# Splitting the first expert layer of a fused attention and mixture kernel into three single TensorE passes

## The chip, the cores and the metric

The kernel runs on one core of one Trainium2 chip. The metric is the device time of one execution in microseconds (us). A single execution carries 1 or 2 us more than the profiled span, which runs from the first to the last instruction. In the lines of the profile PE is TensorE, PEld its weight loads, DVE VectorE, ACT ScalarE, POOL GpSimd, and L12 is line 12 of the kernel.

## The reference, cut to what matters

A gated linear attention over 768 steps (4 batches, 8 heads of 48) gives `x` with 3072 rows of 384. Four experts then work on every row:

```python
p = domain_probs / (domain_probs.sum(-1, keepdims=True) + 1e-09)
for e in range(E):                              # E = 4
    h = np.maximum(x @ w1[e], 0.0)              # 384 -> 1024, the layer that the change rewrites
    out += p[:, e:e + 1] * (h @ w2[e])          # 1024 -> 384
```

All inputs are float32.

## The kernel before

The rows are handled in seven token groups: two of 256 rows (groups 0 and 1) and five of 512. While the experts of one group run, the attention of the next group is interleaved with them, a piece at a time. An "up" is one 128-row block of the first layer, a "down" is one 128-row block of the second. All weights are loaded once and stay in SBUF.

```python
w1_sb = const.tile([P, E, KC, F], F32, name="w1_sb")
w2_sb = const.tile([P, E, FCH, DM], F32, name="w2_sb")
...
def up(gi, e, fc):
    n = len(groups[gi]) * P                      # 256 or 512
    ...
    hps = ps.tile([P, NT], F32, name="hps", tag="g")
    for kc in range(KC):                         # KC = 3
        nc.tensor.matmul(hps[:, :n], lhsT=w1_sb[:, e, kc, fc * P:(fc + 1) * P],
                         rhs=xTs[gi][:, kc, :n], start=(kc == 0), stop=(kc == KC - 1))
    nc.scalar.activation(out=hidden[gi, e][:, fc, :n], in_=hps[:, :n], func=ACT.Relu)

def down(gi, e, slot):
    ...
    ops = ps.tile([P, DM], F32, name="ops", tag="o")          # two buffers
    for fc in range(FCH):                        # FCH = 8
        nc.tensor.matmul(ops, lhsT=hT[:, fc, slot * P:(slot + 1) * P], rhs=w2_sb[:, e, fc, :], ...)
    # VectorE: acc = ops * prob + acc; after the last expert, DMA to out
```

One of seven levels of an attention unit looks as follows. TensorE computes the scores, then VectorE updates `QT`, `KT` and the decays. The next level's scores need those three, so a level is a chain TensorE, VectorE, TensorE.

```python
for li, m in enumerate(LEVELS):
    # 8 small matmuls sc <- KT, QT (16 instructions in the profile)
    nc.vector.tensor_mul(qv[:, :, :, 1, :], qv[:, :, :, 1, :], spread(left))    # QT
    nc.vector.tensor_mul(kv[:, :, :, 0, :], kv[:, :, :, 0, :], spread(right))   # KT
    nc.vector.tensor_mul(dec, left, right)
    # two copy_predicated lat <- sc
    yield                                        # here other work is placed between
```

## Time and profile before

The median of three runs was 1429.11 us (1428.98 to 1430.6); the profiled execution spans 1426.1 us.

| stage | length, us | TensorE busy, us | granted clock |
|---|---|---|---|
| prologue (attention of the first two units, loads) | 77.6 | 50.0 | 0.63 |
| group 0 (256 rows) | 103.4 | 101.3 | 1.00 |
| group 1 (256 rows) | 173.8 | 158.1 | 0.92 |
| groups 2 to 5 together (512 rows each) | 882.0 | 876.2 | 1.00 |
| group 6 (512 rows, no attention beside it) | 189.3 | 185.7 | 1.00 |

How to read it: length less busy time is TensorE's idle time. The clock is the mean that the throttle granted, 1.00 being full speed; where a trace has no record of it, the views show 1.00. Busy time is not a fixed quantity, because the same instructions are busy longer at half clock.

### The profile page before, as it was taken

Reading aid. Unit: us, or ns where it says so; the run is one execution under the profiler, and the core shown is the slowest. Engines: PE = TensorE matmul, PEld = TensorE weight load, DVE = VectorE, ACT = ScalarE, POOL = GpSimd, SP = SyncE. Lnnn points to the kernel's source line nnn. Section 1 sums busy time; section 2 is a strip of 40 time slices with the busy share of each in tenths; the row PEclk is TensorE's granted clock in tenths of the full one; section 3 lists DMA queues with packets and bytes.
Section 4 is the critical chain, followed back from the end, with each engine's and each line's share of the span. In section 5 each row is a group of like instructions: output and inputs, shape, how many; then the busy total and the mean of one; then the engine's idle time right before and its main releaser. Section 6 shows DMA issues by size and latency. Waiting matters only on the chain.

```text
span 1426.1 us, 16040 instructions
## 1 busy us (share of the span) xinstructions
PE 1371.2 (96%) x6712; PEld 858.4 (60%) x6712; DVE 421.7 (30%) x1086; ACT 169.0 (12%) x317; POOL 55.8 (4%) x128
## 2 busy tenths in 40 slices
PE   5799989989999999999999999999999999999998
PEld 4677776667556556566566565565565565555555
DVE  4343244433332322333323223323233233000001
ACT  1021111110110110110101101101101011101110
POOL 2000000000000000000000000000000000000000
PEclk7599998998999999999999999999999999999999
DMA  9421002110020010020110020100001000000000
GB/s 312 130 45 23 1 7 50 23 23 6 7 45 6 18 23 5 2 62 0 23 23 1 6 50 12 23 6 18 6 18 28 1 1 1 0 23 0 0 0 23
DMA packets 112504, 37.39 MB, mean 26 GB/s; under 512 B 103600, under 2 KB 110896, under 8 KB 112432
## 3 DMA queue, kind: packets, MB, share of 16 engines
q1 hardware_dynamic: 109056, 36.18, 10.1%
q8 instruction: 54, 0.88, 0.3%
q10 hardware_dynamic: 3376, 0.17, 0.2%
q14 instruction: 18, 0.15, 0.0%
HBM read 31.63 MB, written 4.72 MB: 25 GB/s over the span
## 4 chain that ended last, share of the span: by engine, by line
PE 95%; DVE 3%; issue 1%; DMA 0%; SPq 0%; ACT 0%; ACTq 0%
PE hps L226 36%; PE ops L235 35%; PE sc L162 14%; PE tp L128 3%; PE yps L187 3%; PE yps L184 1%; PE sps L198 1%; DVE lat L174 1%; DVE KT L169 1%; PE xps L215 1%; DVE QT L168 0%; DMA ra<-in_alpha_dram 0%; DVE dec L171 0%; SPq L102 0%; ACT xT L216 0%
## 5 line engine op out<-in xcount | busy, mean ns | idle before, releaser
L226 PE MATMUL hps<-xT,w_sb 128*128 128x512 f32 (+1 forms) x1344 | 543.1, 546 | 1.7 <-ACT xT L216 1.7
L235 PE MATMUL ops<-w_sb,hT 128*128 128x384 f32 x1536 | 510.8, 488 | 0.0
L235 PEld LDWEIGHTS ops<-w_sb,hT 128*128 128x128 f32 x1536 | 286.6, 190 | 188.5 <-issue 2.4
L226 PEld LDWEIGHTS hps<-xT,w_sb 128*128 128x128 f32 x1344 | 244.9, 192 | 191.5 <-issue 169.3
L162 PEld LDWEIGHTS sc<-QT,KT 48*128 48x128 f32 x2688 | 190.5, 202 | 135.2 <-issue 132.0
L162 PE MATMUL sc<-QT,KT 48*128 48x64 f32 x2688 | 215.4, 294 | 34.4 <-DVE lat L174 34.4
L228 ACT ACTIVATE hT<-hps 128x512 f32<-128x512 f32 (+1 forms) x224 | 120.2, 536 | 782.0 <-PE hps L226 782.0
L243 DVE SCALAR_TENSOR_TENSOR acc<-ops,p_all,acc 128x384 f32<-128x384 f32 x72 | 44.5, 618 | 391.4 <-PE ops L235 391.4
L174 DVE COPY_PREDICATED lat<-masks,sc 128x256 f32<-128x256 uint8 x336 | 152.7, 519 | 0.0
L168 DVE TENSOR_TENSOR QT<-QT,dec 128x256 f32<-128x256 f32 x144 | 61.3, 426 | 263.5 <-PE sc L162 263.5
L151 POOL TENSOR_TENSOR own<-rv,dot 128x384 f32<-128x384 f32 x24 | 19.9, 830 | 1049.8 <-DVE dot L150 942.2
L169 DVE TENSOR_TENSOR KT<-KT,dec 128x256 f32<-128x256 f32 x144 | 60.3, 419 | 0.0
L187 PE MATMUL yps<-rv,lat 128*128 128x48 f32 x384 | 56.4, 278 | 0.0
L187 PEld LDWEIGHTS yps<-rv,lat 128*128 128x128 f32 x384 | 52.9, 204 | 0.2
L240 DVE TENSOR_SCALAR acc<-ops,p_all 128x384 f32<-128x384 f32 x24 | 14.8, 618 | 124.8 <-PE ops L235 124.8
L194 ACT COPY AT<-tp 128x512 f32<-128x512 f32 x20 | 11.7, 586 | 281.6 <-PE tp L128 281.4
L144 DVE TENSOR_TENSOR QT<-tp,AT 128x512 f32<-128x512 f32 x24 | 16.6, 692 | 85.8 <-PE tp L128 85.8
L184 PE MATMUL yps<-st,QT 128*128 128x96 f32 x160 | 32.8, 286 | 0.0
L189 DVE TENSOR_TENSOR own<-own,yps 128x384 f32<-128x384 f32 x24 | 13.3, 554 | 64.0 <-PE yps L187 64.0
L184 PEld LDWEIGHTS yps<-st,QT 128*128 128x128 f32 x160 | 25.8, 192 | 5.5 <-issue 2.4
L171 DVE TENSOR_TENSOR dec<-dec 128x128 f32<-128x128 f32 (+3 forms) x144 | 28.1, 195 | 0.0
L149 POOL TENSOR_TENSOR own<-rq,rk 128x384 f32<-128x384 f32 x24 | 24.6, 1024 | 64.6 <-PE xps L215 60.3
(36 smaller groups left out, 301.3 us busy)
## 6 DMA issues: line engine op xcount, KB each, us to landing
w_sb<-in_moe_w_dram SPq DMA_DIRECT2D x8, 1536.0 KB, 16.2
ra<-in_alpha_dram SPq DMA_DIRECT2D x24, 192.0 KB, 2.8
rk<-in_k_dram SPq DMA_DIRECT2D x24, 192.0 KB, 3.3
rq<-in_q_dram SPq DMA_DIRECT2D x24, 192.0 KB, 3.4
rv<-in_v_dram SPq DMA_DIRECT2D x24, 192.0 KB, 2.7
out_dram<-acc SPq DMA_DIRECT2D x24, 192.0 KB, 1.9
ident<-ident_c ACTq DMA_DIRECT2D x1, 64.0 KB, 1.8
masks<-masks_c ACTq DMA_DIRECT2D x1, 56.0 KB, 2.5
```

Source lines behind the costliest of these rows:

```text
L128: nc.tensor.transpose(tp[:, p, :], src(p), ident)
L162: nc.tensor.matmul(sc[i][:, p, :], lhsT=KT[rows, p, :], rhs=qv[rows, p, :, 1, :], start=True, stop=True)
L168: nc.vector.tensor_mul(qv[:, :, :, 1, :], qv[:, :, :, 1, :], spread(left))
L169: nc.vector.tensor_mul(kv[:, :, :, 0, :], kv[:, :, :, 0, :], spread(right))
L171: nc.vector.tensor_mul(dec, left, right)
L174: nc.vector.copy_predicated(halves(lat[:, i], m)[:, :, :, 1, :], mk.unsqueeze(1).broadcast_to([P, NP, nb, m]), sc[i].rearrange("p a (b r) ...
L184: nc.tensor.matmul(yps[:, p], lhsT=QT[:, p, :], rhs=st[:, p], start=True, stop=False)
L187: nc.tensor.matmul(yps[:, p, i, :], lhsT=lat[:, i, p, :], rhs=rv[:, 2 * p + i, :], start=(cb == 0), stop=(cb == 0 or i == 1))
L226: nc.tensor.matmul(hps[:, :n], lhsT=w1_sb[:, e, kc, fc * P:(fc + 1) * P], rhs=xTs[gi][:, kc, :n], start=(kc == 0), stop=(kc == KC - 1))
L228: nc.scalar.activation(out=hidden[gi, e][:, fc, :n], in_=hps[:, :n], func=ACT.Relu)
L235: nc.tensor.matmul(ops, lhsT=hT[:, fc, slot * P:(slot + 1) * P], rhs=w2_sb[:, e, fc, :], start=(fc == 0), stop=(fc == FCH - 1))
L243: nc.vector.scalar_tensor_tensor(out=acc, in0=ops, scalar=prob, in1=acc, op0=ALU.mult, op1=ALU.add)
```

## The change

A float32 matmul of 512 columns takes 2 x 429 ns in this kernel. The change computes the same product from three single passes whose operands fit the narrower single-pass form (float32r in the code). Write x = H + L and w = A + B, where H and A are the values with their low 12 bits cleared. The kernel keeps A, 4096·B and A - 4096·B of the weights, and H, L and H/4096 - L of x. It accumulates `one` = A·H + 4096·B·L and `two` = (A - 4096·B)·(H/4096 - L). Then `one`·(1 + 1/4096) - `two` is, apart from rounding, A·H + A·L + B·H + B·L: four products for three multiplications.

The price: w1 grows threefold and no longer fits in SBUF beside everything else. So each half expert (a "piece") is split on chip once, written to DRAM as `kept`, and read back for every later group; w2 is read from DRAM each time too. The core of the diff (cuts marked):

```diff
+    def split_weights(i):
+        w = w1t[i] = wts.tile([P, 3, KC, FH], F32R, name="w1")      # wts: two buffers
+        r = staged.pop(i)
+        top = wts.tile([P, KC, FH], F32, name="w_top", bufs=1)
+        nc.scalar.activation(out=r, in_=r, func=ACT.Copy, scale=4096.0)
+        clear_low(top, r)                                           # VectorE bit mask
+        nc.scalar.activation(out=w[:, 0], in_=top, func=ACT.Copy, scale=1 / 4096.0)
+        nc.gpsimd.tensor_sub(w[:, 1], r, top)
+        nc.gpsimd.tensor_sub(w[:, 2], w[:, 0].bitcast(F32), w[:, 1].bitcast(F32))
+        nc.sync.dma_start(out=kept[i], in_=w.bitcast(F32))
+    def load_w1(i):
+        if i < NPC:                                                 # the 8 pieces of the first group
+            split_weights(i)
+        elif i < NPC * len(groups):
+            w = w1t[i] = wts.tile([P, 3, KC, FH], F32R, name="w1")
+            nc.sync.dma_start(out=w.bitcast(F32), in_=kept[i % NPC])
...  # attention: x is split the same way, one ScalarE and three VectorE operations a unit
     def up(gi, e, fc):
...
+        if f == 0:                                                  # first of a piece's four ups
+            if i > 0:
+                stage(i + 3)
+                load_w1(i + 1)
...
-        for kc in range(KC):
-            nc.tensor.matmul(hps[:, :n], lhsT=w1_sb[:, e, kc, fc * P:(fc + 1) * P], ...
-        nc.scalar.activation(out=hidden[gi, e][:, fc, :n], in_=hps[:, :n], func=ACT.Relu)
+        for out, parts in ((one, (1, 0)), (two, (2,))):
+            for part in parts:
+                for kc in range(KC):
+                    nc.tensor.matmul(out, lhsT=w1t[i][:, part, kc, col], ...
+        nc.scalar.activation(out=t, in_=one, func=ACT.Copy, scale=1 + 1 / 4096.0)
+        nc.vector.tensor_sub(hT, t, two)
...  # relu on ScalarE, one up later
+        if f == FPH - 1:
+            del w1t[i]
     def down(gi, e, slot):
-        ops = ps.tile([P, DM], F32, name="ops", tag="o")
+        ops = ps.tile([P, DM], F32, name="ops", tag="o", bufs=1)
```

More of the change, by code (lines that the diff above doesn't have):

```diff
@@ L11 @@
 F32 = mybir.dt.float32
+F32R = mybir.dt.float32r
+U32 = mybir.dt.uint32
 U8 = mybir.dt.uint8
@@ L54 @@
     NT = B * P
+    HALVES = 2
+    FH = F // HALVES
+    FPH = FCH // HALVES
+    NPC = E * HALVES
     LEVELS = [1 << i for i in range(7)]
@@ L66 @@
     const = ctx.enter_context(tc.tile_pool(name="const", bufs=1))
-    raw = ctx.enter_context(tc.tile_pool(name="raw", bufs=3))
+    wts = ctx.enter_context(tc.tile_pool(name="wts", bufs=2))
+    dram = ctx.enter_context(tc.tile_pool(name="dram", bufs=1, space=bass.MemoryType.DRAM))
     work = ctx.enter_context(tc.tile_pool(name="work", bufs=2))
@@ L73 @@
     masks = const.tile([P, len(LEVELS), HALF], U8, name="masks")
-    w1_sb = const.tile([P, E, KC, F], F32, name="w1_sb")
-    w2_sb = const.tile([P, E, FCH, DM], F32, name="w2_sb")
     NBLK = B * NCB
@@ L87, with load @@
     place = {u: (gi, i) for gi, g in enumerate(groups) for i, u in enumerate(g)}
-    raws = {}
+    srcs = {"a": alpha, "k": k, "q": q, "v": v}
+    raws = [{nm: const.tile([P, H, D if nm == "v" else HD], F32, name=f"r{nm}{i}")
+             for nm in srcs} for i in range(2)]
     xTs = {}
     hidden = {}
+    relus = deque()
     accs = {}
-    def load(u):
+    def load(u, names):
         if u >= len(units):
@@ L97, in load @@
         cb, b = units[u]
-        for nm, src in (("a", alpha), ("k", k), ("q", q)):
-            t = raw.tile([P, NP, 2, HD], F32, name=f"r{nm}")
-            flat = t.rearrange("p a b c -> p (a b) c")
-            nc.gpsimd.memset(flat[:, :, D:], 0.0)
+        for nm in names:
             nc.sync.dma_start(
-                out=flat[:, :, :D],
-                in_=src[b, :, cb * P:(cb + 1) * P, :].rearrange("h s d -> s h d"))
-            raws[u, nm] = t
-        t = raw.tile([P, H, D], F32, name="rv")
@@ L107, in load @@
-        nc.sync.dma_start(
-            out=t, in_=v[b, :, cb * P:(cb + 1) * P, :].rearrange("h s d -> s h d"))
-        raws[u, "v"] = t
-    def load_weights(e):
-        nc.sync.dma_start(out=w1_sb[:, e], in_=moe_w1[e].rearrange("(c p) f -> p c f", p=P))
-        nc.sync.dma_start(out=w2_sb[:, e], in_=moe_w2[e].rearrange("(c p) d -> p c d", p=P))
+                out=raws[u % 2][nm][:, :, :D],
+                in_=srcs[nm][b, :, cb * P:(cb + 1) * P, :].rearrange("h s d -> s h d"))
+    kept = [dram.tile([P, 3, KC, FH], F32, name=f"kept{i}") for i in range(NPC)]
@@ new lines, with stage @@
+    w1t = {}
+    w2t = {}
+    staged = {}
+    def stage(i):
+        if i < NPC:
+            e, h = divmod(i, HALVES)
+            t = staged[i] = wts.tile([P, KC, FH], F32, name="w_raw")
+            nc.sync.dma_start(out=t, in_=moe_w1[e].rearrange(
+                "(c p) f -> p c f", p=P)[:, :, h * FH:(h + 1) * FH])
+    def split_weights(i):
[8 more added lines that the diff above has]
+        nc.sync.dma_start(out=kept[i], in_=w.bitcast(F32))
@@ new lines, in load_w1, with load_w2, clear_low @@
+    def load_w1(i):
+        if i < NPC:
+            split_weights(i)
+        elif i < NPC * len(groups):
+            w = w1t[i] = wts.tile([P, 3, KC, FH], F32R, name="w1")
+            nc.sync.dma_start(out=w.bitcast(F32), in_=kept[i % NPC])
+    def load_w2(j):
+        if j < E * len(groups):
+            t = w2t[j] = wts.tile([P, FCH, DM], F32, name="w2")
+            nc.sync.dma_start(out=t, in_=moe_w2[j % E].rearrange("(c p) d -> p c d", p=P))
+    def clear_low(out, in_):
+        nc.vector.tensor_scalar(out=out.bitcast(U32), in0=in_.bitcast(U32), scalar1=0xFFFFF000,
+                                scalar2=None, op0=ALU.bitwise_and)
@@ L132, in attention @@
         cb, b = units[u]
-        load(u + 2)
-        ra, rk, rq, rv = (raws.pop((u, nm)) for nm in ("a", "k", "q", "v"))
+        ra, rk, rq, rv = (raws[u % 2][nm] for nm in ("a", "k", "q", "v"))
         lat = lats[u % 2]
-        heads = lambda t: t.rearrange("p a b c -> p (a b) c")[:, :, :D]
-        pair = lambda t: lambda p: t[:, p].rearrange("p b c -> p (b c)")
+        heads = lambda t: t[:, :, :D]
+        pair = lambda t: lambda p: t[:, 2 * p:2 * p + 2, :].rearrange("p b c -> p (b c)")
         AT = work.tile([P, NP, P], F32, name="AT")
@@ L151, in attention @@
         nc.gpsimd.tensor_mul(own, rv, dot.unsqueeze(2).broadcast_to([P, H, D]))
+        load(u + 2, "akq")
         yield
@@ L207, in attention @@
                     nc.vector.tensor_add(old, old, add)
+        load(u + 2, "v")
         gi, slot = place[cb, b]
         if slot == 0:
-            xTs[gi] = work.tile([P, KC, NT], F32, name="xT")
+            xTs[gi] = work.tile([P, 3, KC, NT], F32R, name="xT")
         xps = ps.tile([P, KC, P], F32, name="xps", tag="w")
@@ L215, in attention @@
             nc.tensor.transpose(xps[:, c, :], flat[:, c * P:(c + 1) * P], ident)
-        nc.scalar.copy(out=xTs[gi][:, :, slot * P:(slot + 1) * P], in_=xps)
+        xH, xL, xD = (xTs[gi][:, part, :, slot * P:(slot + 1) * P] for part in range(3))
+        top = work.tile([P, KC, P], F32, name="x_top")
+        clear_low(top, xps)
+        nc.scalar.copy(out=xH, in_=top)
+        nc.vector.tensor_sub(xL, xps, top)
+        nc.vector.scalar_tensor_tensor(out=xD, in0=top, scalar=1 / 4096.0, in1=xL.bitcast(F32),
+                                       op0=ALU.mult, op1=ALU.subtract)
         yield
@@ L221, in up @@
         n = len(groups[gi]) * P
-        if fc == 0:
-            hidden[gi, e] = hid.tile([P, FCH, NT], F32, name="hT")
-        hps = ps.tile([P, NT], F32, name="hps", tag="g")
-        for kc in range(KC):
-            nc.tensor.matmul(hps[:, :n], lhsT=w1_sb[:, e, kc, fc * P:(fc + 1) * P],
-                             rhs=xTs[gi][:, kc, :n], start=(kc == 0), stop=(kc == KC - 1))
-        nc.scalar.activation(out=hidden[gi, e][:, fc, :n], in_=hps[:, :n], func=ACT.Relu)
+        h, f = divmod(fc, FPH)
@@ new lines, in up @@
+        i = gi * NPC + e * HALVES + h
+        if f == 0:
+            if i > 0:
+                stage(i + 3)
+                load_w1(i + 1)
+            hidden[gi, e, h] = hid.tile([P, FPH, NT], F32, name="hT", bufs=3)
+        hT = hidden[gi, e, h][:, f, :n]
+        one, two = (ps.tile([P, NT], F32, name=f"hps{j}", tag="g", bufs=3)[:, :n] for j in range(2))
+        col = slice(f * P, (f + 1) * P)
+        for out, parts in ((one, (1, 0)), (two, (2,))):
+            for part in parts:
+                for kc in range(KC):
+                    nc.tensor.matmul(out, lhsT=w1t[i][:, part, kc, col],
+                                     rhs=xTs[gi][:, part, kc, :n],
+                                     start=(part == parts[0] and kc == 0),
+                                     stop=(part == parts[-1] and kc == KC - 1))
@@ L230, in down @@
+        t = work.tile([P, NT], F32, name="t")[:, :n]
+        nc.scalar.activation(out=t, in_=one, func=ACT.Copy, scale=1 + 1 / 4096.0)
+        nc.vector.tensor_sub(hT, t, two)
+        relus.append(hT)
+        while len(relus) > (0 if fc == FCH - 1 else 1):
+            r = relus.popleft()
+            nc.scalar.activation(out=r, in_=r, func=ACT.Relu)
+        if f == FPH - 1:
+            del w1t[i]
     def down(gi, e, slot):
         cb, b = groups[gi][slot]
-        hT = hidden[gi, e]
-        ops = ps.tile([P, DM], F32, name="ops", tag="o")
+        w2 = w2t[gi * E + e]
@@ L234, in down @@
+        ops = ps.tile([P, DM], F32, name="ops", tag="o", bufs=1)
         for fc in range(FCH):
-            nc.tensor.matmul(ops, lhsT=hT[:, fc, slot * P:(slot + 1) * P], rhs=w2_sb[:, e, fc, :],
-                             start=(fc == 0), stop=(fc == FCH - 1))
+            h, f = divmod(fc, FPH)
+            nc.tensor.matmul(ops, lhsT=hidden[gi, e, h][:, f, slot * P:(slot + 1) * P],
+                             rhs=w2[:, fc, :], start=(fc == 0), stop=(fc == FCH - 1))
         prob = p_all[:, b * NCB + cb, e:e + 1]
@@ L253 @@
         nc.scalar.dma_start(out=p_all, in_=moe_domain_probs.rearrange("(n p) e -> p n e", p=P))
+        for r in raws:
+            for nm in "akq":
+                nc.gpsimd.memset(r[nm][:, :, D:], 0.0)
         for t in lats:
@@ L257 @@
             nc.gpsimd.memset(t, 0.0)
-        load(0)
-        load(1)
-        for e in range(E):
-            load_weights(e)
+        load(0, "akqv")
+        load(1, "akqv")
+        stage(0)
+        stage(1)
+        load_w2(0)
         live = [attention(u) for u in range(len(groups[0]))]
+        rounds = 0
         while live:
             live = [g for g in live if next(g, live) is not live]
+            rounds += 1
+            if rounds in (4, 6):
+                stage(2 + len(w1t))
+                load_w1(len(w1t))
         norm_probs()
@@ L292 @@
                     step, due = pieces / (E * (FCH + len(groups[gi])) - 2), 0.0
-                for fc in range(FCH):
+                for fc in range(FPH):
                     up(gi, e, fc)
@@ L298 @@
                     down(*seq[i - 1], slot)
+                    advance()
+            load_w2(i + 1)
+            if i < len(seq):
+                for fc in range(FPH, FCH):
+                    up(gi, e, fc)
                     advance()
```

## The prediction

> **What bounds the kernel now.** I read the page first (busy shares, slices, chain of waits), then summed the engines over the eight stages of the program (the prologue, then the seven token groups, cut at the first up-matmul of each), then timelines of single stretches.
>
> ```profile
> PE 1371.2 (96%) x6712; PEld 858.4 (60%) x6712; DVE 421.7 (30%) x1086; ACT 169.0 (12%) x317; POOL 55.8 (4%) x128
> ...
> PEclk7599998998999999999999999999999999999999
> ...
> PE 95%; DVE 3%; issue 1%; DMA 0%; SPq 0%; ACT 0%; ACTq 0%
> PE hps L226 36%; PE ops L235 35%; PE sc L162 14%; PE tp L128 3%; PE yps L187 3%; PE yps L184 1%; PE sps L198 1%; DVE lat L174 1%; DVE KT L169 1%; PE xps L215 1%; DVE QT L168 0%; DMA ra<-in_alpha_dram 0%; DVE dec L171 0%; SPq L102 0%; ACT xT L216 0%
> ```
>
> TensorE is the bound: 95% of the chain is its own work, 36% the first expert layer (hps), which the change rewrites. The stages are not alike, though:
>
> ```profile
> 0.00:77.60 77.60, 49.95 (x310) 44.88 (x310) 31.59 (x83) 5.76 (x9) 8.46 (x28) 0.63 0.69 208
> 77.60:181.00 103.40, 101.25 (x598) 77.55 (x598) 33.70 (x90) 16.57 (x40) 4.46 (x10) 1.00 0.10 20
> 181.00:354.80 173.80, 158.10 (x972) 122.00 (x973) 68.05 (x175) 20.75 (x48) 9.43 (x20) 0.92 0.11 22
> 354.80:569.40 214.60, 212.71 (x1069) 125.86 (x1067) 69.50 (x182) 27.13 (x48) 8.92 (x20) 1.00 0.08 16
> 569.40:793.70 224.30, 222.98 (x1101) 132.17 (x1102) 70.22 (x184) 27.34 (x48) 8.94 (x20) 1.00 0.09 19
> 793.70:1017.80 224.10, 222.81 (x1102) 132.00 (x1100) 70.48 (x184) 27.35 (x48) 8.92 (x20) 1.00 0.08 18
> 1017.80:1236.80 219.00, 217.67 (x1054) 126.85 (x1053) 65.23 (x168) 25.00 (x44) 6.64 (x10) 1.00 0.03 8
> 1236.80:1426.10 189.30, 185.72 (x513) 97.05 (x511) 12.98 (x21) 19.11 (x32) 0.00 (x0) 1.00 0.02 9
> ```
>
> The columns are stretch, length, then busy time of PE, weight load, DVE, ACT, POOL, granted clock, DMA share, GB/s. In the prologue PE is a third idle at clock 0.63; group 1 (third row) idles too and its clock sags to 0.92; all others are full of PE work. The last group has no attention beside it, so its timeline gives the bare price of an up-matmul:
>
> ```profile
> 1236.76 20.76 PE L226 MATMUL hps<-xT,w_sb 128*128 128x512 f32 x48
> 1257.36 3.07 PE L235 MATMUL ops<-w_sb,hT 128*128 128x384 f32 x9
> ```
>
> From start to start, 20.60 us over 48 instructions are 429 ns each. A 512-column float32 matmul is two such instructions, and an up (three of them) takes 6 x 429 = 2.58 us. Where attention is interleaved, one level looks like this:
>
> ```profile
> 701.18 2.84 PE L226 MATMUL hps<-xT,w_sb 128*128 128x512 f32 x6
> 701.32 0.43 DVE L168 TENSOR_TENSOR QT<-QT,dec 128x256 f32<-128x256 f32 x1 [2.25 <-PE sc L162]
> 701.66 0.42 DVE L169 TENSOR_TENSOR KT<-KT,dec 128x256 f32<-128x256 f32 x1
> ...
> 702.10 0.76 DVE L174 COPY_PREDICATED lat<-masks,sc 128x256 f32<-128x256 uint8 x2
> ...
> 703.95 1.11 PE L162 MATMUL sc<-QT,KT 48*128 48x64 f32 x16
> ```
>
> The vector work of a level ends at 702.86, 1.1 us before the next level's scores start. That slack is what a shorter up eats. Two more lines matter below, the only place in the page's data where GpSimd and VectorE collide, and the rate of DMA while all weights stream in:
>
> ```profile
> 187.15 1.13 POOL L149 TENSOR_TENSOR own<-rq,rk 128x384 f32<-128x384 f32 x1
> 187.33 1.23 DVE L169 TENSOR_TENSOR KT<-KT,AT 128x256 f32<-128x256 f32 x1
> ```
>
> ```profile
> 14.00:42.00 28.00, 16.17 (x111) 14.97 (x111) 13.84 (x35) 0.00 (x0) 0.85 (x4) 0.54 1.04 391
> ```
>
> **What the Trainium skill says.** "FP8 and Floating Point Precision", TensorE Precision Notes: true FP32 is four passes, and the reduced form reads four bytes and truncates to FP22, natively held; so 12-bit parts in one pass each are plausible. "TensorE: Matmul & The Clock Gate", section "Wait — 56ns, not 53.3ns?": matmuls back to back start N / 2.4 + 2.5 ns apart at full clock. Two passes of 512 columns give 429 ns, exactly what the trace shows; one pass gives 216 ns, 109 ns at 256 columns. "SBUF — State Buffer", Who interferes with whom: a VectorE instruction with two SBUF inputs contends with a GpSimd instruction that reads SBUF, and one waits for the whole of the other. The trace agrees: KT above took 1.23 us beside the GpSimd product, 0.42 us elsewhere. "GPSIMD Engine Reference", 3.1 Elementwise: about 2.6 cycles an element for a tensor_tensor. The trace has 830 ns for 384 elements (row L151), so four times that, 3.3 us, for the 1536 elements of a weight split (estimate).
>
> **The change, part by part.**
>
> *Removed.* An up is now nine single passes. At 512 columns: 9 x 216 = 1.94 us instead of 2.58, 0.63 us less, over 160 ups (five groups of 32): 101 us. At 256 columns: 9 x 109 = 0.98 instead of 6 x 216 = 1.30, over 64 ups: 20 us. Together 121 us. In group 1 two thirds of the ups stand beside attention levels whose chain of scores, VectorE, scores already sets the pace; I take 6 us off: 115 us gained. Weight loads (107 to 112 ns apart at best in the trace's short matmuls) hide under 216 ns.
>
> *Vector and scalar work per up* (a copy of about 0.60 us, a subtract of about 0.69 like row L144, a relu) falls into the 1.2 us in which VectorE waits for the next scores. ACT has 1.2 us per up, DVE 0.7 + 1.5 per level, against an up plus a level of about 3.1 us on PE. Only the two widest levels (VectorE chain 2.2 to 2.3 us instead of 1.5) no longer fit, by about 0.3 us, perhaps 13 times: +4 us. The new x split (three VectorE operations of about 0.5 us per unit) sits at the ends of groups: +5 us.
>
> *Splitting w1 on chip*, eight pieces. Each is an ACT scale (1.45 us, from 384 and 597 ns at 256 and 512 columns), a VectorE mask of 0.9 to 1.8 us, an ACT scale back, and two GpSimd subtracts of 3.3 us. The subtracts lock out QT, KT and dec, on which the scores hang. Two pieces are split in the prologue, which is a chain of exactly those: up to 6 us each, +12. Six are split in group 0 while PE works on the piece before; four ups with their levels are about 7 us of PE, the split takes 10 to 12, and ACT's copies queue behind it: 4 us each, +25.
>
> *w1 reloaded.* From group 1 on, each half expert (3 x 3 x 512 floats a partition, 2.36 MB) comes back from DRAM, and w2 (1.57 MB) too. Total traffic is some 0.2 GB, 150 GB/s, against 391 shown. The average is harmless, the window is not: the next expert's first half is queued behind the w2 load, which waits for the last down of the expert before. Both then take 1.9 (a lone 192 KB load lands after 2.8, of which about 1 is data) + 3.93 MB / 391 GB/s = 10.0, so about 12 us, within four ups. With attention those are 13.6 to 15 us from the last down: no wait, save at the end of each group, where the pieces run out (about 11): 4 x 1.4, and 3 at the start of group 1, so +9 us. In the last group four bare ups are 7.8 us: about 4.5 us, three times: +14.
>
> *One ops buffer instead of two.* A down after a down now waits for the accumulate: 0.49 us until the last matmul is out, 0.62 for DVE (row L243), two hand-overs, so 1.2 us from its last start instead of 0.32. With a level of scores in between (1.04 us) it is covered; in the order of the changed program 15 downs of the last group stand bare: 15 x 0.87 = +13 us.
>
> Sum: -115 + 4 + 5 + 12 + 25 + 9 + 14 + 13 = -33 us, so 1429 - 33 = 1396; I say 1397 us.
>
> **The rivals.** (a) *All of the gain lands* (about 1315): if splits and reloads hide. For it: DVE and ACT are at 30% and 12%. Against: the window arithmetic and the lock, both local. (b) *The reload binds everywhere*: were the kept pieces to move at 300 GB/s, both loads need 15 us and each of some 20 windows loses 1 to 3 us more: 1420 to 1440. For it: peak rate was seen only in one stretch. Against: that stretch had 1.5 to 4 KB rows, these are 18 KB. (c) *The single pass is no single pass*: at 429 ns each an up would take 3.9 us, over 200 us worse, about 1640. Nothing in this trace has such a matmul; the skill's wording speaks against it. (d) *The clock sags in the early groups*: in the prologue PE at a third idle was granted 0.63. If the stalls of group 0 do that, its PE work of some 90 us stretches: 1410 to 1435. (e) *PSUM*: three buffers for two tiles per up; but each is read out within an up, so I expect no wait.
>
> **Range and chances.** The gain of 115 is firm if the pass rate is; the costs (82 us) are estimates good to perhaps 30 us together, split and clock weighing most. Range 1360 to 1435. The 2% line is at 1400.5, close to my figure: faster 0.54, within 2% 0.37, slower 0.09.
>
> **What would show each step.** Nine up-matmuls starting 216 ns apart in the last group; stage sums with about 197 to 208 us in the full groups, prologue near 90, group 0 near 120, last group longer than before (near 197) in spite of cheaper ups. PE waiting on GpSimd's w1 in group 0, QT or KT of over 2 us beside the subtracts, PE waiting on the DMA of w1 about 4.5 us three times at the end, on acc 15 times. Wrong if up-matmuls start over 216 ns apart, if full groups don't get shorter, or if the splits turn out hidden.

## The result and the profile after

The changed kernel is correct and slower: 1482.11 us in the median of four runs (1481.71 to 1487.23), against 1429.84 for the kernel before beside it. The ratio is 1.0374, with a 95% interval of 1.035 to 1.0398. Here and below a ratio is the mean time of one kernel's fast runs over that of the other's in the same rounds, so it is not quite the ratio of the medians. The prediction said 1397 and a range up to 1435: it missed the direction as well as the range.

The page of the changed kernel, to be set beside the three lines that open the prediction (engines' busy time, granted clock in 40 slices, chain that ended last):

```profile
PE 1339.3 (90%) x7384; PEld 990.1 (67%) x7384; DVE 629.2 (43%) x1390; ACT 295.3 (20%) x557; POOL 101.8 (7%) x78
...
PEclk7567868989799999999999999999999999999999
...
PE 81%; DMA 7%; DVE 6%; issue 3%; ACT 2%; SPq 0%; ACTq 0%; DVEq 0%
PE ops L307 35%; PE hps L287 24%; PE sc L207 14%; DMA w<-kept 7%; PE yps L232 3%; PE tp L173 2%; DVE KT L214 1%; PE yps L229 1%; DVE lat L219 1%; DVE QT L213 1%; PE sps L243 1%; ACT t L292 1%; ACT AT L186 1%; DVE acc L315 1%; DVE hT L293 1%
```

Two things are to be seen. The first layer (hps) did shrink, from 36% to 24% of the chain, but TensorE's busy time fell by only 32 us in all. And TensorE now owns 81% of the chain instead of 95%: the kept weights' DMA, VectorE and ScalarE have come in. The clock is down in most of the slices 3 to 11, up to a quarter into the program, where it was mostly full before.

The same stages as the prediction shows for the kernel before (stretch, length, then busy time of PE, weight load, DVE, ACT, POOL, granted clock, DMA share, GB/s):

```profile
0.00:90.66 90.66, 51.94 (x310) 46.37 (x311) 46.75 (x90) 11.64 (x13) 21.29 (x23) 0.59 0.48 141
90.66:243.38 152.72, 120.34 (x694) 98.46 (x695) 72.41 (x135) 42.96 (x84) 45.58 (x16) 0.78 0.52 184
243.38:425.79 182.41, 160.89 (x1068) 130.42 (x1069) 86.31 (x220) 30.61 (x80) 7.21 (x8) 0.86 0.46 157
425.79:629.17 203.38, 199.05 (x1165) 145.37 (x1165) 97.22 (x226) 43.93 (x80) 7.19 (x8) 0.99 0.42 142
629.17:843.34 214.17, 210.65 (x1197) 152.28 (x1197) 99.53 (x229) 43.54 (x80) 7.17 (x8) 0.99 0.40 136
843.34:1054.84 211.50, 208.80 (x1197) 151.12 (x1197) 98.44 (x228) 43.38 (x80) 7.19 (x8) 1.00 0.41 138
1054.84:1266.45 211.61, 203.84 (x1148) 145.71 (x1149) 94.17 (x213) 43.07 (x78) 6.22 (x7) 1.00 0.38 135
1266.45:1480.40 213.95, 183.78 (x608) 120.35 (x608) 34.36 (x52) 36.17 (x64) 0.00 (x0) 0.94 0.26 103
```

| stage | before | after | difference | what the prediction's terms give |
|---|---|---|---|---|
| prologue | 77.6 | 90.7 | +13 | near 90 |
| group 0 | 103.4 | 152.7 | +49 | near 120 |
| group 1 | 173.8 | 182.4 | +9 | about 175 (4 off, which is 10 less the 6 for the chain; some 5 of small costs back) |
| groups 2 to 5 | 882.0 | 840.7 | -41 | about 816 (20 off each, some 3.5 of small costs back) |
| group 6 | 189.3 | 214.0 | +25 | near 197 |

The full groups do get shorter, so the idea works where nothing disturbs it. What it wins there, 41 us, group 0 alone takes back. Read group 0's row closely: TensorE is idle for 152.7 - 120.3 = 32 us, and its busy time itself rose to 120.3 us although the ups there are cheaper; the clock stands at 0.78. In group 6 the idle time is 30 us and the clock 0.94.

What TensorE waited for in the whole changed kernel (total us, times, longest):

```profile
PE sc L207 <- DVE lat L219: 56.3, 34, 6.7
PE hps L287 <- DMA w<-kept: 30.4, 8, 5.7
...
PE hps L287 <- ACT t L292: 12.6, 8, 3.2
PE ops L307 <- DVE acc L315: 9.6, 14, 0.7
```

Before, the only large one was the first, with 34.4 us and at most 2.6. The weight split in group 0 shows how it grew. This is the timeline of the changed kernel, all engines, from there (start, duration, engine and line, what, how often, idle time before and its cause):

```profile
106.57 3.46 POOL L141 TENSOR_TENSOR w<-w 128x1536 fp32r<-128x1536 f32 x1
...
107.88 2.43 DVE L213 TENSOR_TENSOR QT<-QT,dec 128x256 f32<-128x256 f32 x1 [1.45 <-PE sc L207]
...
111.63 2.50 PE L207 MATMUL sc<-QT,KT 48*128 48x64 f32 x16 [1.60 <-DVE lat L219]
...
118.20 1.22 PE L207 MATMUL sc<-QT,KT 48*128 48x64 f32 x16
...
119.84 1.48 ACT L139 ACTIVATE w<-w_top 128x1536 fp32r<-128x1536 f32 x1 [1.15 <-PE sc L207]
...
121.23 0.64 ACT L292 ACTIVATE t<-hps 128x256 f32<-128x256 f32 x2
...
121.65 2.46 PEld L287 LDWEIGHTS hps<-xT,w 128*128 128x128 f32 x12 [1.54 <-ACT t L292]
...
123.44 3.48 POOL L141 TENSOR_TENSOR w<-w 128x1536 fp32r<-128x1536 f32 x1
123.56 3.64 DVE L214 TENSOR_TENSOR KT<-KT,dec 128x256 f32<-128x256 f32 x1
```

`QT` took 2.43 us and `KT` 3.64 instead of 0.42, each ending with the GpSimd subtract that it overlaps (107.88 + 2.43 is 0.3 us after 106.57 + 3.46; `KT` and the second subtract end within 0.3 us of each other). The `t` copy that frees an up's PSUM buffer stands behind the split's scaling on ScalarE, and TensorE waits for it. The scores at 111.63 took 2.50 us for the same 16 matmuls that take 1.22 at 118.20: half clock, as the trace's clock record says (0.5 from 104.8 to 118.5 us).

Group 6 from its timeline (TensorE only), beside the two lines of the same spot in the prediction:

```profile
1266.45 11.14 PE L287 MATMUL hps<-xT,w 128*128 128x512 f32 x36 [4.86 <-DMA w<-kept]
1277.43 5.33 PE L307 MATMUL ops<-w,hT 128*128 128x384 f32 x16
1283.47 5.43 PE L307 MATMUL ops<-w,hT 128*128 128x384 f32 x16 [0.71 <-DVE acc L315]
...
1300.72 8.70 PE L287 MATMUL hps<-xT,w 128*128 128x512 f32 x36
1314.77 10.90 PE L287 MATMUL hps<-xT,w 128*128 128x512 f32 x36 [5.36 <-DMA w<-kept]
```

36 up-matmuls run in 8.70 us when nothing came before, but in 10.90 after a wait of 5.36 us. In the records of the single matmuls, the first 10 to 13 after each such wait start 427 ns apart, the others 229. The clock record of the trace reads 0.5 for 6.8 us at each of these four places. So a wait here costs 5.4 us itself, and 2.0 to 2.4 us of half speed afterwards.

One long wait isn't needed for that. In group 1 of the kernel before, the clock fell too, and no wait there was longer than 1.8 us (first line: waits of the scores in that group, total us, times, longest; then the 3.4 us before one of its two falls, and the stretch after it, as in the stage table):

```profile
PE sc L162 <- DVE lat L174: 12.9, 16, 1.8
...
227.80:231.20 3.40, 1.97 (x16) 1.42 (x16) 2.80 (x5) 0.38 (x1) 0.99 (x1) 1.00 0.60 119
231.20:244.90 13.70, 11.92 (x62) 9.44 (x62) 5.25 (x15) 0.77 (x2) 0.00 (x0) 0.50 0.00 1
```

TensorE was busy for 1.97 of 3.40 us, with waits of 1.26 and 0.16 us. Set against the clock records, the twelve traces have 161 falls of the clock, each after 3.4 us in which TensorE was busy for 0.8 of the time or less, whether through one wait or several. Not every stretch like that lowered it: some 250 of them, down to a busy share of 0.45, did not.

### The profile page after: what moved, and what is told of

The parts are those of the page before. It is cut to its first block, busy times and chain, and to the rows that moved or that the text cites. A ratio compares the mean times of both kernels' runs of the same rounds, so it can differ in the third digit from the quotient of the medians.

```text
span 1480.4 us, 18451 instructions
## 1 busy us (share of the span) xinstructions
PE 1339.3 (90%) x7384; PEld 990.1 (67%) x7384; DVE 629.2 (43%) x1390; ACT 295.3 (20%) x557; POOL 101.8 (7%) x78
## 4 chain that ended last, share of the span: by engine, by line
PE 81%; DMA 7%; DVE 6%; issue 3%; ACT 2%; SPq 0%; ACTq 0%; DVEq 0%
PE ops L307 35%; PE hps L287 24%; PE sc L207 14%; DMA w<-kept 7%; PE yps L232 3%; PE tp L173 2%; DVE KT L214 1%; PE yps L229 1%; DVE lat L219 1%; DVE QT L213 1%; PE sps L243 1%; ACT t L292 1%; ACT AT L186 1%; DVE acc L315 1%; DVE hT L293 1%
## 5 line engine op out<-in xcount | busy, mean ns | idle before, releaser
L307 PE MATMUL ops<-w,hT 128*128 128x384 f32 x1536 | 529.5, 499 | 11.7 <-DVE acc L315 9.6
L287 PE MATMUL hps<-xT,w 128*128 128x512 f32 (+1 forms) x2016 | 481.6, 391 | 46.8 <-DMA w<-kept 30.4
L287 PEld LDWEIGHTS hps<-xT,w 128*128 128x128 f32 x2016 | 362.4, 207 | 113.7 <-issue 33.5
L307 PEld LDWEIGHTS ops<-w,hT 128*128 128x128 f32 x1536 | 289.2, 193 | 209.8 <-DVE acc L315 17.9
L292 ACT ACTIVATE t<-hps 128x512 f32<-128x512 f32 (+1 forms) x224 | 119.6, 535 | 944.4 <-PE hps L287 944.3
L293 DVE TENSOR_TENSOR hT<-t,hps 128x512 f32<-128x512 f32 (+1 forms) x224 | 136.7, 611 | 232.9 <-PE hps L287 122.1
L297 ACT ACTIVATE hT<-hT 128x512 f32<-128x512 f32 (+1 forms) x224 | 126.0, 563 | 17.2 <-DVE hT L293 17.0
L214 DVE TENSOR_TENSOR KT<-KT,dec 128x256 f32<-128x256 f32 x144 | 74.0, 514 | 0.0
L312 DVE TENSOR_SCALAR acc<-ops,p_all 128x384 f32<-128x384 f32 x24 | 14.8, 617 | 99.5 <-PE ops L307 99.5
L140 POOL TENSOR_TENSOR w<-w_raw,w_top 128x1536 fp32r<-128x1536 f32 x8 | 27.6, 3446 | 101.7 <-PE hps L287 51.6
L173 PE MATMUL tp<-ident,rq 128*128 128x128 f32 x96 | 17.7, 312 | 15.0 <-ACT AT L186 13.7
## 6 DMA issues: line engine op xcount, KB each, us to landing
w<-kept SPq DMA_DIRECT2D x48, 2304.0 KB, 11.8
```

The lines of the kernel that those rows point to most:

```text
L287: nc.tensor.matmul(out, lhsT=w1t[i][:, part, kc, col], rhs=xTs[gi][:, part, kc, :n], start=(part == parts[0] and kc == 0), stop=(part == p ...
L292: nc.scalar.activation(out=t, in_=one, func=ACT.Copy, scale=1 + 1 / 4096.0)
L293: nc.vector.tensor_sub(hT, t, two)
L297: nc.scalar.activation(out=r, in_=r, func=ACT.Relu)
L307: nc.tensor.matmul(ops, lhsT=hidden[gi, e, h][:, f, slot * P:(slot + 1) * P], rhs=w2[:, fc, :], start=(fc == 0), stop=(fc == FCH - 1))
```

## The experiments

My first account after reading the result: (1) group 0 loses through the splits, by the lock between GpSimd and VectorE and by ScalarE's order; (2) group 6 loses through the late reload; (3) single passes start 229 ns apart, not 216. The rival to (1) was that the clock sags for another reason and the splits merely stand beside it; the rival to (3), that the DMA traffic or the weight loads slow the matmuls. Experiments 1 to 4 shared one chip and its runs of the kernel before, 5 to 8 another, 9 and 10 a third. All times below are medians.

### One piece split, the others not (wrong result)

```diff
     def stage(i):
-        if i < NPC:
+        if i == 0:
...
     def load_w1(i):
-        if i < NPC:
+        if i == 0:
             split_weights(i)
...
-            nc.sync.dma_start(out=w.bitcast(F32), in_=kept[i % NPC])
+            nc.sync.dma_start(out=w.bitcast(F32), in_=kept[0])
...
-                load_w1(i + 1)              # at the first up of a piece
...
             del w1t[i]
+            load_w1(i + 2)                  # as soon as the buffer is free
```

> Only the first half expert is split on chip; the other seven are read back from the one kept piece (wrong values on purpose), and every reload is issued as soon as its buffer is free, as in the early-reload run of this batch. Theory: the seven splits (GpSimd locking VectorE, ACT held up, and the half clock that PE falls to in those stalls) cost the prologue about 6 us and group 0 about 50 us, so against the early-reload run this one is 50 to 60 us shorter, near 1390 us, and group 0 falls from 152.7 to about 95 to 100 us at a granted clock near 1. Rival: group 0 is slow because its short ups leave PE waiting for the attention chain whatever the split does; then it stays above 130 us and the whole above 1425.

1393.97 us, ratio 0.9739 (0.9711 to 0.9767). All pieces are read from the one that was split, so the values are wrong (relative error 1.08), while the instructions of TensorE are those of the changed kernel. Groups 0, 1 and 6 of this run:

```profile
85.48:188.71 103.23, 99.72 (x694) 81.98 (x694) 49.17 (x129) 26.77 (x72) 3.59 (x4) 0.94 0.69 241
188.71:373.00 184.29, 165.69 (x1069) 134.81 (x1069) 86.45 (x220) 29.72 (x78) 7.21 (x8) 0.83 0.46 155
1204.97:1392.35 187.38, 173.34 (x609) 113.45 (x607) 35.04 (x53) 37.51 (x67) 0.00 (x0) 1.00 0.33 122
```

Group 0 fell to 103.2 us, a little above the 95 to 100 expected. This kernel also reloads earlier, so its proper partner is the kernel after next, which has the same early reloads.

### The splits' subtracts on VectorE instead of GpSimd

```diff
-        nc.gpsimd.tensor_sub(w[:, 1], r, top)
-        nc.gpsimd.tensor_sub(w[:, 2], w[:, 0].bitcast(F32), w[:, 1].bitcast(F32))
+        nc.vector.tensor_sub(w[:, 1], r, top)
+        nc.vector.tensor_sub(w[:, 2], w[:, 0].bitcast(F32), w[:, 1].bitcast(F32))
```

> The two subtracts of each split move from GpSimd to VectorE (about 1.75 us each from VectorE's 1.06 ns a column, instead of 3.45). Theory of the lock: QT and KT no longer wait for a whole GpSimd instruction (up to 3.6 us twice per split), VectorE is held 3.5 us in place of about 6; prologue minus 5 us, group 0 minus 15 to 25, total near 1458. Rival, that the order of work on ACT (the scale back waits for the mask, and the copies of the up results queue behind it) makes the stalls: then within 5 us of the changed kernel.

Correct, 1453.92 us, ratio 1.0166 (1.0142 to 1.019): 28 us faster than the changed kernel. The prologue lost 6 us and group 0 13, less than the 15 to 25 expected. The vector instructions of group 0 by line (count, busy us and mean ns), first in the changed kernel, then here:

```profile
L213 DVE TENSOR_TENSOR QT<-QT,dec 128x256 f32<-128x256 f32 x12 | 12.3, 1027 | 11.1 <-PE sc L207 11.1
L214 DVE TENSOR_TENSOR KT<-KT,dec 128x256 f32<-128x256 f32 x12 | 12.3, 1021 | 0.0
```

```profile
L140 DVE TENSOR_TENSOR w<-w_raw,w_top 128x1536 fp32r<-128x1536 f32 x6 | 10.5, 1758 | 0.2
...
L213 DVE TENSOR_TENSOR QT<-QT,dec 128x256 f32<-128x256 f32 x12 | 5.1, 423 | 8.6 <-PE sc L207 8.6
L214 DVE TENSOR_TENSOR KT<-KT,dec 128x256 f32<-128x256 f32 x12 | 5.0, 418 | 0.0
```

`QT` and `KT` are back at 0.42 us. The subtract takes 1.76 us on VectorE against 3.45 on GpSimd, and locks out nobody. So the lock is shown. But group 0 is still at 139.7 us, far above 103: the lock is the smaller part of what the splits do there. TensorE's waits for `lat` in group 0 fell from 11.7 to 3.8 us, those for the `t` copy only from 12.1 to 11.1. What ScalarE's order alone costs was not tested.

### Reload as soon as the buffer is free

```diff
-                load_w1(i + 1)
+                if i + 1 < NPC:
+                    load_w1(i + 1)          # splits: unchanged
...
             del w1t[i]
+            if i + 2 >= NPC:
+                load_w1(i + 2)              # reloads: at the last up of a piece
```

> The reload of a w1 piece is issued right after the last up of the piece that held its buffer, ahead of the downs and of the w2 load, instead of after them; all else as in the changed kernel, exact result. Theory: the four waits of about 5 us in the last group go and with them the half clock that follows each (13 matmuls at 427 instead of 229 ns, 2.6 us), so the last group falls from 214 to about 183 us and groups 3 to 5 lose 2 to 5 us each: total near 1443. Rival, that the traffic itself (207 MB) slows the core wherever it is: no change over 5 us, the waits move elsewhere.

Correct, 1452.07 us, ratio 1.0148 (1.0123 to 1.0172). It is 9 us above the expected 1443, because of group 1. No wait of an up for kept weights is left. Groups 0, 1 and 6:

```profile
90.46:239.17 148.71, 120.37 (x694) 98.48 (x694) 71.91 (x135) 42.98 (x84) 45.60 (x16) 0.78 0.53 188
239.17:432.60 193.43, 174.30 (x1068) 142.19 (x1068) 87.53 (x220) 29.73 (x78) 7.23 (x8) 0.79 0.45 148
1262.87:1450.75 187.88, 173.80 (x609) 113.57 (x607) 35.05 (x53) 37.52 (x67) 0.00 (x0) 1.00 0.34 122
```

Group 6 fell from 214.0 to 187.9 us. Of these 26 us, 16 are idle time (30.2 to 14.1), which are the three waits of 5.4 us inside the group. The other 10 are busy time (183.8 to 173.8) for the same instructions, with the clock back at 1.00: nearly all of it the half speed after each of the four waits. Groups 2 to 5 together lost 10 us. Group 1, however, became 11 us *longer*, and its clock fell from 0.86 to 0.79; I come back to that.

Now the pair of this kernel and the first: in group 0 only the splits differ, and the reads that stand in for them (148.7 against 103.2 us). The same 694 matmuls were busy for 120.4 us with the splits and 99.7 without, and idle for 28.3 and 3.5 us. So the splits cost 45.5 us there: 25 of waiting, and 21 of longer TensorE work with the clock at 0.78 instead of 0.94. In time of the whole program the pair differs by 58 us, the rest lying in the prologue (5) and group 1 (9). The rival, that the clock sags for another reason, is refuted for the larger part: without the splits it is 0.94.

### Two buffers for the down of the last group

```diff
-        ops = ps.tile([P, DM], F32, name="ops", tag="o", bufs=1)
+        if gi == len(groups) - 1:
+            ops = ps.tile([P, DM], F32, name="ops", tag="w")      # the attention's two, idle by then
+        else:
+            ops = ps.tile([P, DM], F32, name="ops", tag="o", bufs=1)
```

> In the last group, where no attention runs, the down results alternate between the two PSUM buffers that attention used, instead of the single ops buffer. Theory: 15 waits of 0.87 us go, minus 13 us, total near 1469, no wait of ops on acc left there. Rival: the DMA of w1 absorbs it (the four reload waits get longer by what is gained, since the window starts at the last down): minus 4 us or less; as the reload is queued behind the w2 load that waits for the same last down, I expect no such absorption.

Correct, 1466.44 us, ratio 1.0269 (1.0227 to 1.0311). Group 6 is 14.8 us shorter, where the prediction had worked out 13 for these waits. Twelve of the 15 waits went; three of 0.71 us stayed, against the expectation, since the downs at the head of this stage belong to group 5 and keep the single buffer. About 3 of the 14.8 us are not the buffer's: the ups after the four reload waits took 9.84 to 10.23 us instead of 10.74 to 11.14, the half speed being shorter in this execution.

```profile
1265.32:1464.44 199.12, 177.52 (x608) 119.07 (x608) 34.34 (x52) 36.19 (x64) 0.00 (x0) 0.94 0.28 111
```

### What a single pass costs, measured alone

```diff
+        # after the last group: 36 matmuls each of nine weights/nine movers, one/one,
+        # nine weights/one mover, one weight/nine movers; then 36 in bfloat16
+        for pick_w, pick_x in ((turn, turn), (same, same), (turn, same), (same, turn)):
+            t = dst()
+            for j in range(36):
+                ...
+                nc.tensor.matmul(t, lhsT=w[:, a, c, :P], rhs=x[:, b, d, :], start=True, stop=True)
```

> The changed kernel with five rows of 36 matmuls of 512 columns appended after the last down, results thrown away: single-pass with nine weights and nine moving operands in turn (as in an up), with one weight and one moving operand, nine weights and one moving operand, one weight and nine moving operands, and last bfloat16 with nine weights. In the changed kernel an up-matmul starts every 229 ns at full clock where one pass of 512 columns should take 216. If the extra 13 ns belong to the single-pass float32 form itself, the first four rows all show about 229 and bfloat16 216; if they come from the change of weights, only rows with nine weights show it; if from the moving operand, only rows with nine moving operands; if from DMA or other traffic in the kernel, all rows show 216, as nothing else runs then.

Correct; one run, whose total is not compared. The tail in TensorE's timeline:

```profile
1481.58 33.43 PE L402 MATMUL probe<-xT,w 128*128 128x512 f32 x144
1514.85 7.94 PE L405 MATMUL probe<-xb,wb 128*128 128x512 bf16 x35
```

From start to start, the median is 229 ns in each of the four float32r rows (repeating 226, 229, 232), whether weights or movers change or not, with no DMA running. In bfloat16 it is 216. So the 13 ns belong to the single-pass float32 form itself, and both rivals to (3) fall.

### Fillers against the clock: transposes

In each attention level of the first eight units, eight identity transposes are put after the scores, to see whether more TensorE activity brings the clock back and the time with it.

```diff
+            if u < 8:
+                warm = ps.tile([P, P], F32, name="warm", tag="o", bufs=1)
+                for _ in range(8):
+                    nc.tensor.transpose(warm, ident, ident)
             yield
```

> The changed kernel with eight 128-column transposes of the identity after each level of scores in the prologue and groups 0 and 1 (56 levels, results thrown away), to keep PE active while it waits for VectorE. Theory: the half clock granted in these stages (mean 0.59, 0.78, 0.86) stretches both PE's work and, through the scores, the attention chain; with the filler the clock stays near 1 and the prologue falls by about 10 us, group 0 by 10 to 20, group 1 by about 10, total 1440 to 1455, although PE has 49 us more work at full clock. Rival: the clock follows from stalls but costs nothing, since VectorE and the splits set the pace; then the time is the same or longer by part of the 49 us.

Correct, 1486.47 us, ratio 1.0391 (1.0367 to 1.0415). The clock rose from 0.78 to 0.87 in group 0 and from 0.86 to 0.94 in group 1, and yet both stages were 5 us longer. The fillers cost more than the clock gave back. Of the 124.8 us that TensorE was busy in group 0 here, 16 to 19 are fillers (by how overlapping instructions are counted), so the rest took 106 to 109 us instead of 120.3: the low clock does cost TensorE time. But the idle time stayed at 32.5 us. In the prologue the scores stayed at half clock (1.97 us for 16).

### All repairs together

The edits of the second and the fourth kernel, and splits as well as reloads issued as soon as a buffer is free:

```diff
-            if i > 0:
-                stage(i + 3)
-                load_w1(i + 1)
...
             del w1t[i]
+            stage(i + 4)
+            load_w1(i + 2)
```

> Exact result: subtracts of the split on VectorE, split and reload of a piece issued as soon as its buffer is free (before the downs), and two PSUM buffers for the downs of the last group. If the three causes add up: last group 214 minus 26 minus 15 = 173 to 175, prologue 85, group 0 near 125 (the split of every other piece now lies beside downs), total 1395 to 1405, so 2% faster than the kernel before. Rival, that they overlap: above 1420.

Correct, 1412.02 us in the median of six runs (1403.28 to 1413.49), ratio 0.9862 (0.9836 to 0.9888): 70 us faster than the changed kernel, and the fastest correct version of all here, 1.4% under the kernel before (within the 2% that count as the same). The expected 1395 to 1405 was missed, mainly through group 1, which at 190.3 us is 8 longer than in the changed kernel. Groups 0, 1 and 6:

```profile
84.66:213.52 128.86, 110.08 (x694) 90.43 (x694) 75.56 (x147) 43.43 (x84) 3.59 (x4) 0.87 0.61 217
213.52:403.79 190.27, 171.44 (x1068) 140.10 (x1069) 86.49 (x220) 29.80 (x78) 7.21 (x8) 0.80 0.45 150
1235.85:1411.54 175.69, 170.13 (x609) 114.44 (x607) 35.06 (x53) 37.57 (x67) 0.00 (x0) 1.00 0.36 130
```

Group 6 is now 14 us shorter than before the change, and idle for 5.6 us only. Group 0 is still 26 us above the kernel with one split: 15 of idle time, 10 of slower work.

### The same with transposes, and with real matmuls as fillers

First the repaired kernel with the eight transposes a level of above:

> The run before with the filler transposes as well. Theory of the clock: another 20 to 40 us less in the prologue and groups 0 and 1, total 1365 to 1385. Rival: no change or longer.

1418.84 us, ratio 0.9919 (0.9901 to 0.9936), correct: on the same chip, 7 us slower than without them. Group 0 took 139.9 us, group 1 184.1.

Then four float32 matmuls of 128 columns in place of the transposes, in the first eight units, and in the first two units alone (the prologue):

```diff
+            if u < 8:                       # second version: u < 2
+                warm = ps.tile([P, P], F32, name="warm", tag="o", bufs=1)
+                for _ in range(4):
+                    nc.tensor.matmul(warm, lhsT=ident, rhs=ident, start=True, stop=True)
```

> The kernel with the three repairs together plus four real 128-column float32 matmuls of the identity after each level in the prologue and groups 0 and 1. With eight transposes instead, PE was never idle in the prologue and its scores still ran at half clock (1.98 us for 16). If transposes do not count for the clock and matmuls do, the prologue now reaches full clock (scores 1.1 us) and falls from 84.7 to 70 to 78 us, and groups 0 and 1 (128.9 and 190.3) lose 10 to 25 us together: near 1385 us. Rival: the clock answers to something else, or the 36 us of filler that is not hidden eats the gain: 1410 to 1425 us as with the transposes.

> The same filler in the prologue alone. If full clock can be had there, 7 to 15 us less than the three repairs together (1412), near 1400, with groups 0 and 1 as they were; if not, 1412 or slightly more.

("Never idle" in the first text holds for stretches only: TensorE was busy for 74.8 of the 92.7 us of the first filler kernel's prologue.) Both are correct: 1417.29 us (ratio 0.9916, 0.9893 to 0.9939) and 1415.83 us (0.9903, 0.9883 to 0.9923). Neither beats the repaired kernel's 0.9862. Groups 0 and 1 of the version for eight units, to be read beside the two first rows of the repaired kernel:

```profile
87.24:223.75 136.51, 117.82 (x806) 98.59 (x807) 75.88 (x147) 43.46 (x84) 3.59 (x4) 0.92 0.57 205
223.75:406.81 183.06, 171.76 (x1292) 142.57 (x1293) 87.91 (x220) 29.72 (x78) 7.16 (x8) 0.96 0.47 156
```

In group 1 the clock rose from 0.80 to 0.96 and the stage lost 7 us; in group 0 it rose from 0.87 to 0.92 and the stage became 8 us longer: TensorE's idle time there stayed at 18.7 us, and the fillers added more work than the clock returned. And the prologue of the same run, TensorE only:

```profile
33.75 1.97 PE L207 MATMUL sc<-QT,KT 48*128 48x64 f32 x16
35.65 2.07 PE L226 MATMUL warm<-ident 128*128 128x128 f32 x8
37.65 1.97 PE L207 MATMUL sc<-QT,KT 48*128 48x64 f32 x16
39.56 2.07 PE L226 MATMUL warm<-ident 128*128 128x128 f32 x8
```

TensorE is busy without a break here, in fact from 9.4 to 41.6 us, and the scores still take 1.97 us for 16 rather than the 1.11 of the level shown in the prediction. (The clock record of this run begins at 82.6 us only, so it says nothing here; in the run with fillers in the prologue alone it reads 0.5 with the same 1.97 us.) What the clock answers to in this stretch stays open.

## Why the prediction was wrong, by its own steps

The prediction is 85 us short. By stage: group 0 some 33, the full groups 25, group 6 17, group 1 7, the prologue none; the rest is rounding.

- **"Six are split in group 0 ... 4 us each, +25" is the step that failed.** The mechanism that it named, subtracts that lock out `QT` and `KT` and ScalarE copies that queue, is there (2.43, 3.64 us; ups waiting on `t` for 12.1 us in group 0). The idle time of 25 us, from the pair with and without splits, even fits. What the sum left out is that these pauses lower the clock: another 21 us of slower work at 0.78. TensorE waited for the `t` copies and the scores, never for GpSimd's w1 itself, which the prediction had among its signs. The prediction held the clock as rival (d), "if the stalls of group 0 do that", outside the sum. It was not an alternative to the stalls but came with them. Then, the 10 us that 32 cheaper ups were to save in group 0 never arrived: even with one split, group 0 took 103.2 us against 103.4 before. TensorE was idle there for only 3.5 us (2.2 before), so it is not the chain of levels that took them. By the measured pitch of a pass the ups could save 7.5; the clock, at half speed for 13 of the 103 us, cost some 6.5 (estimate), and 1.3 went to longer waits.
- **"One pass gives 216 ns, 109 ns at 256 columns" was mis-sized.** A single float32 pass took 229 and about 118 ns, so one of the prediction's own signs of being wrong (over 216 ns apart) came true. An up of 512 columns saves 2.57 - 9 x 0.229 = 0.51 us instead of 0.63, one of 256 columns 1.30 - 1.06 = 0.23 instead of 0.31. Over 160 and 64 ups this makes 98 us instead of 121. This accounts for about 15 of the 25 us missing in groups 2 to 5.
- **Reload waits at the ends of groups** came to more than the 9 us put down: 5.67 us at the start of group 1, then 2.30, 1.14 and 0.32, and 4.86 just before group 6. Reloading early brought 10 us in groups 2 to 5. Some 5 us of the shortfall in the full groups I cannot assign.
- **"About 4.5 us, three times: +14" in the last group** was nearly right as a wait (5.36, 5.39, 5.36 us), and wrong as a cost: the half clock after each of the four waits, one of them just before the group, added 10 us, shown by the early reload. The Trainium skill, "TensorE: Matmul & The Clock Gate", Part 1, gives an idle window of about 3.4 us after which the clock is halved. The prediction cited this page for the pitch and did not ask of its own 4.5-us waits whether they pass that window. The trace agrees here: half clock for 6.8 us, twice 3.4, after each of these waits, none after the 0.7-us waits for `acc`. It isn't the whole rule, as the falls without any long wait in the two kernels' group 1 show.
- **"One ops buffer ... +13 us" was right**: 14.8 us came back with a second buffer, about 3 of them by a shorter half speed and the rest by 12 of the 15 waits.
- **The prologue, +12, was right** (13.1 measured); moving the subtracts to VectorE returned 6 of it.
- **Group 1** was to gain 4 us on its ups, 10 less 6 for the chain of levels, and lost 9. Its length follows the clock more than the edits: 182 us at 0.86, 184 at 0.83, 190 at 0.80, 193 at 0.79, although the fillers show that a higher clock bought by extra work isn't worth its price. With the early reload the clock falls six times in this group, each time after 3.4 us in which TensorE was busy for only 0.5 to 0.7 of the time, in waits of at most 1.8 us, mostly of the scores for `lat`. Why the half speed lasts longer after these falls (10.2 to 20.5 us) than in the changed kernel (mostly 3.4 to 10.2), I could not settle.
- **Rivals:** (a) fell. So did (b): the waits are local, the kept pieces land after 11.8 us in the median, queued behind w2. (c) fell, for an up is shorter; (e) showed only as the wait for `t` in group 0, which goes with the splits (12.1 us with them, 0.5 in the whole run with one); that ScalarE's order causes it is read from the timeline, not tested. (d) came true as part of the main case.

## What to carry to other kernels

When you price a stall on TensorE, add the half speed that can follow it: those measured here, of about 5 us, cost 7 to 8, because the next 10 to 13 matmuls ran at half speed. Count short waits together, too: the clock fell in these runs after 3.4 us in which TensorE was busy for 0.8 of the time or less, also where no single wait was longer than 1.8 us. A preparation that runs "on other engines" is only free if those engines aren't links of the chain that feeds TensorE and don't lock one that is: here six splits cost 45 us in a stage where the cheaper ups were to save 10. Issue a reload where its buffer becomes free, not where the next piece is begun; with that, subtracts on the faster engine and a second accumulator buffer, the same idea went from 3.7% slower to 1.4% faster.

## What the Trainium skill lacked or had wrong

- "TensorE: Matmul & The Clock Gate", section on the 56 ns, has no price for single-pass float32. Its N / 2.4 + 2.5 ns holds for bfloat16 here (216 ns at 512 columns), but single-pass float32 starts every 229 ns (226, 229, 232 in turn), and about 118 ns at 256 columns. At half clock single-pass float32 is as the page says (427 ns at 512 columns); bfloat16 was not measured there.
- The same page, Part 1, says that a sustained busy window of about 3.4 us frees the clock. In the prologue of the kernel with float32 fillers TensorE was busy without a break for 32 us, with scores of 48 rows and 64 columns and float32 matmuls of 128 columns, and stayed at half speed (1.97 us for 16 scores instead of 1.11). In group 1 of the early reload it was busy for all of the 10.3 us from 247.9 us on, at a clock of 0.50. Part 4 says that transposes don't count as busy in the same way; which other matmuls count is missing. And in group 1 transposes as fillers went with a clock of 0.95, matmuls with 0.96, against 0.80 without: no difference between the two showed there.
- How idle TensorE must be for its clock to fall, no page says. Here it fell 161 times in twelve traces, each time after 3.4 us with a busy share of 0.8 or less, and stayed up after some 250 such stretches ("TensorE: Matmul & The Clock Gate" is where it belongs). The half speed is dear when it recurs: the four waits of group 6 cost 10 us of it.
- "GPSIMD Engine Reference", 3.1, was slightly low for the long subtracts: 2.6 cycles an element makes 3.3 us for 1536 elements (estimate), measured were 3.44 to 3.48. For 384 elements it fits (0.83 us).
